# Batch 0's channel output in one 64x64 run per cycle: seventh to ninth cycle of an attention and token/channel mixer kernel

## Chip, cores and metric

The kernel runs on one core of a Trainium2 chip. The metric is the device time of one execution in microseconds (us), the median of several runs. Matmuls run on TensorE (PE in the profile, its weight loads PEld), element-wise work on VectorE (DVE) and ScalarE (ACT), casting loads from memory are issued by GpSimd (POOL), transposing copies and stores by SyncE (SP).

## What is computed

```python
scores = scale * np.matmul(q, k.transpose(0, 1, 3, 2)) - np.log(S)
attn = 1.0 / (1.0 + np.exp(-scores))
x = np.matmul(attn, v)            # then heads side by side: (8, 448, 768)
xt = x.transpose(0, 2, 1)
h = np.maximum(xt @ w_tok1, 0.0) @ w_tok2
u = x + h.transpose(0, 2, 1)
h2 = np.maximum(u @ w_ch1, 0.0) @ w_ch2
return u + h2
```

q, k and v are (8, 12, 448, 64) in float32: 8 batches, 12 heads, 448 positions, head size 64. `w_tok1` is 448x256, `w_tok2` 256x448, `w_ch1` 768x1536, `w_ch2` 1536x768. The output is (8, 448, 768) in float32. The kernel multiplies in fp16 and accumulates in fp32.

## The kernel before

The work is cut into 24 cycles `c`, three per batch (`c = 3*b + u`); a cycle takes four heads. In each cycle seven score steps `qk(b, u, j)` (L182) make the scores of one seventh of the keys in four 64x64 quarters of TensorE, all four at once, and ACT applies the sigmoid and writes `att`. `av` (L208) multiplies the previous cycle's `att` with the values, in quarters too, into two accumulators `xa` that DVE copies to `xu`. `xtrans_dma` (L242) transposes `xu` to `xn` by a transfer on SP's queue. For the cycle two back, `tok_tail` (L267) and `tok1` (L285) are the first token product (the tail in quarters, the rest with the whole 128x128 array; ACT applies the ReLU), and `ytrans` (L312) is the second; DVE adds its two results to `xu`.

With a batch's `xu` complete, the channel products follow. `ch1` (L357, batch 0 only) and `sevens` (L1223, a Strassen-like scheme with seven half-size products named 1 to 7 over three column groups a, b, c) make the hidden layer `h2`; `utrans` (L337) and `token_sums` (L447) prepare it. The second channel product gives the output in groups `(t, half)`: 128 tokens by 384 of the 768 columns, for t = 0, 1, 2, and a last one of 64 tokens for both halves. Before the change batch 0's groups are made by `ch2` (L578): twelve 128x128 matmuls of 384 columns each (L586), then three that add `u` through the identity (L597), then a DVE copy (`ch2_out`, L616). The last one is `ch2_last` (L881): 24 matmuls that use 128 rows and 64 columns of the array (L893) and six that add `u` (L904).

PSUM has eight banks: two tiles of two banks each under the tag `qk` (scores, and products ab of `sevens`), and four banks `m0` to `m3` that `bank()` (L88) hands out, first by a list written out by hand (`OPENING_BANKS`, L27), later from the bank set in `at_bank[0]` on, in turn. A bank or a tile can be written again only when its last reader is done. Every engine runs its instructions in the order in which the program issues them; nothing is reordered.

In the sixth cycle (c = 5) two output groups, (0,0) and (1,0), end the cycle (L1202). In cycles seven to nine (c = 6, 7, 8; from here c6, c7, c8), the loop at L1231, the other four groups and the last one are cut into 20 pieces of three steps; `work(share)` (L1242) puts a third of a cycle's share at each of three places between score steps. With each piece goes one waiting piece of DVE work: a re-layout of q or k (`relayout`, L123, through `through_dma`, L147) or a sum of channel weights (`weight_sums`, L424, twelve of them). c8 ends with `sevens` of batch 1. From c9 on, `steady` (L1315) orders the cycles otherwise: scores, values and quarter products stand together in one run.

Of the kernel before, what the change touches and what calls it, by code (L numbers as in the profile page):

```python
# [21 lines left out]
NJ = 7  # L22
# [1 line left out]
NU = 3  # L24
NS = 224
BY_GROUP = [0, 1, 6, 7, 2, 3, 8, 9, 4, 5, 10, 11]
OPENING_BANKS = "2013013013013021302130213021302131302121302130213020213012"  # L27


@with_exitstack  # L30
def kernel(
# [176 lines left out]
    def av(b, u, j0=0, j1=NJ, banks=None):  # L208
        if j0 == 0:
            xa[b, u] = banks or [  # L210
                bank([128, 512], FP32, f"xa_{b}_{u}_{g}")
                for g in range(2)
            ]
        ps = xa[b, u]
        for j in range(j0, j1):
            for g in range(2):
                for hi in range(2):
                    nc.tensor.matmul(  # L218
                        out=ps[g][64 * hi : 64 * hi + 64, 0:S],
                        lhsT=raw[b, "v"][64 * g : 64 * g + 64, u, hi, j, :],  # L220
                        rhs=att[b, u, j][64 * g : 64 * g + 64, hi, :],
                        start=(j == 0),
                        stop=(j == NJ - 1),
                    )
        if j1 == NJ:
            for g in range(2):
                nc.vector.tensor_copy(  # L227
                    out=xu(b)[:, u, g, 0:S], in_=ps[g][:, 0:S]
                )
            if NU * b + u >= N_CYCLES - 2:  # L230
                nc.vector.memset(xu(b)[:, u, :, S:512], 0.0)
            elif NU * b + u >= N_FIRST:
                nc.vector.tensor_copy(
                    out=xu(b)[:, u, :, S:512], in_=xu(b)[:, u, :, S - 64 : S]
                )
# [188 lines left out]
    def weight_sums():  # L424

        low, high = slice(0, NU), slice(NU, NDB)
        first, second = slice(0, MC), slice(MC, CC)
        s1, s2, s4 = sums

        def one(out, in0, in1, op):  # L430
            return [
                lambda d=d: nc.vector.tensor_tensor(
                    out=out[:, d, :], in0=in0[:, d, :], in1=in1[:, d, :], op=op
                )
                for d in range(NU)
            ]
# [225 lines left out]
        turns = [[lambda t=t, n=n: step(t, n) for n in range(n_quads)] for t in range(2)]  # L662
        return turns[0], turns[1], rest

    def split_steps(ps, n_cb, lhsT, rhs):

        def step(n):
            for r in range(2):
                part = slice(64 * r, 64 * r + 64)
                for m in (0, 64):  # L670
                    nc.tensor.matmul(  # L671
                        out=ps[r][m : m + 64, 0:DH],
                        lhsT=lhsT(part, n, m),
                        rhs=rhs(part, n, m),
                        start=(n == 0),
                        stop=(n == n_cb - 1),
                    )

        return [lambda n=n: step(n) for n in range(n_cb)]
# [475 lines left out]
    for c, cb in ((N_FIRST, 3), (N_FIRST + 1, 8)):  # L1155
        b, u = divmod(c, NU)
        before = divmod(c - 1, NU)
        ahead = divmod(c + 1, NU)
        copies = []

        def whole(cb):
            for d in range(0, NDB, 3):
                ch1(0, cb, d, d + 3)
                if copies:
                    copies.pop(0)()

# [24 lines left out]
        if c - 1 not in ON_DMA:  # L1191
            xtrans(*before)
        for t in ("k", "q"):
            pe_transpose(ahead[0], t, ahead[1])
        whole(cb + 3)
        if c == N_FIRST:
            tok1(*before)
            qk(*ahead, 0)
            whole(cb + 4)
            ytrans(*before)  # L1200
        else:
            for w, f in pieces_ch2(0, by_half[:2]):  # L1202
                f()
                if copies:
                    copies.pop(0)()
            while copies:
                copies.pop(0)()

            nc.gpsimd.tensor_copy(out=gate[:, :], in_=tr[2, "q"][:, 1, NJ - 1, 126:128])
            load(2, "v", v, 1, NU)  # L1210
            gated_loads(b)

    pending, copies = [], []

    def some(n):
        for f in copies[:n]:
# [6 lines left out]
    def sevens(b, banks=(2, 3, 0, 1, 0)):  # L1223
        step = ch1_seven(b, banks)
        for at, (n, gs) in enumerate(SEVENS):
            step(n, gs)
            some((2, 0, 1, 1, 1, 1, 1, 1)[at] if at < 8 else 0)

    early = weight_sums()
    lane = [0]  # L1230
    for c in range(2 * NU, ONE_RUN):  # L1231
        b, u = divmod(c, NU)
        before, ahead = divmod(c - 1, NU), divmod(c - 2, NU)


        if c == 2 * NU:
            first = c
            pending, shares = [*pieces_ch2(0, by_half[2:]), *pieces_last(0)], [10, 10, 10]
            total = sum(w for w, f in pending)
            spent = 0  # L1240

        def work(share):  # L1242
            goal = 3 * sum(shares[: c - first]) + share * shares[c - first]
            done = 0
            while pending and spent + done < total * goal / 90:
                w, f = pending.pop(0)
                if len(pending) % 4 == 3:
                    lane[0] ^= 1
                at_bank[0] = 2 + lane[0]
                f()  # L1250
                done += w
                if copies:
                    copies.pop(0)()
                elif early:
                    early.pop(0)()
            return done

        some(len(copies))
        qk(b, u, 0)
        qk(b, u, 1)  # L1260
        at_bank[0] = 0
        av(*before)
        xtrans_dma(*before)
        qk(b, u, 2)
        if c == 2 * NU + 2:
            copies += through_dma(3, 0)[NU + 1 :]
        spent += work(1)
        qk(b, u, 3)
        qk(b, u, 4)
        if u < 2:  # L1270
            at_bank[0] = 0
            tok_tail(*ahead)
            tok1(*ahead, with_scores=True)
        spent += work(2)
        if c == 2 * NU + 2:
            utrans(b - 1)
            token_sums(b - 1)
            spent += work(3)
        qk(b, u, 5)
        qk(b, u, 6)  # L1280
        at_bank[0] = 0
        if u < 2:
            ytrans(*ahead)
        else:
            tok_tail(*ahead)
            tok1(*ahead, with_scores=True)
        if c == 2 * NU + 1:
            copies += through_dma(3, 0)[: NU + 1]
        if u < 2:
            spent += work(3)  # L1290
        if u == 2:
            assert not copies
            extra = output_sums()
            copies += extra[:8]
            del extra[:8]
            sevens(b - 1)
            at_bank[0] = 0
            ytrans(*ahead)
            gated_loads(b)
    assert not copies and not pending and not early  # L1300

    def more(n):
        for f in extra[:n]:
# [203 lines left out]
```

## Time and profile before

| | |
|---|---|
| median of 3 runs | 340.74 us (340.58 to 341.35) |
| profiled execution | 340.27 us |
| its span, first to last instruction | 338.5 us |
| mean granted TensorE clock | 0.998 |
| DVE busy, share of the span | 235.3 us, 70% |
| ACT busy, share of the span | 212.7 us, 63% |
| POOL busy, share of the span | 61.7 us, 18% |

The span is what the trace covers; 1.77 us of the profiled execution lie around it. In a row of the timeline the columns are: start in us from the span's beginning, length in us, engine, line, operation, what is written and read, tile (for a matmul), shape, count; a row can hold several instructions in a row, and a bracket at the end is the idle time ahead of it with what ended it. Matmuls overlap in the pipeline, so the price of one is the distance from its start to the next one's start, not its length.

### The profile page before, as it was taken

The numbers are of one execution on the slowest core, as the hardware profiler recorded it, in microseconds if no ns is written. First come the engines' busy times: TensorE is split into PE (matmuls) and PEld (weight loads), VectorE is DVE, ScalarE is ACT, GpSimd is POOL, SyncE is SP. The second block draws the span as 40 slices with busy tenths as digits, with TensorE's granted clock in tenths as the row PEclk, the third lists the DMA queues.
The fourth block names the chain that finished last, engine by engine and source line by source line (L and its number), as shares of the span: only waits on it lengthen the run. The fifth ranks groups of instructions, "written<-read, shape, count | busy, mean of one in ns | idle before, by whom it ended". The sixth has DMA issues, their size and how long they took to land.

```text
span 338.5 us, 10318 instructions
## 1 busy us (share of the span) xinstructions
PE 332.2 (98%) x4436; PEld 242.9 (72%) x4436; DVE 235.3 (70%) x486; ACT 212.7 (63%) x272; POOL 61.7 (18%) x108
## 2 busy tenths in 40 slices
PE   8999999999999999999999999999999999999994
PEld 5655556555896679767896679766896679769852
DVE  2376466678998874877668774877768653976882
ACT  4996845388747885678647885678657895314200
POOL 8985380050031002020032001110010000000000
PEclk9999999999999999999999999999999999999999
DMA  8999999999999899989998899988993393028006
GB/s 128 162 160 202 207 178 203 175 175 234 186 179 194 158 171 203 182 125 179 186 190 133 152 151 215 201 123 163 195 179 65 67 171 85 2 56 186 4 13 196
DMA packets 103422, 51.91 MB, mean 153 GB/s; under 512 B 75473, under 2 KB 100305, under 8 KB 103377
## 3 DMA queue, kind: packets, MB, share of 16 engines
q1 hardware_dynamic: 77648, 28.84, 47.0%
q0 software_dynamic: 25264, 21.50, 42.4%
q10 hardware_dynamic: 464, 0.92, 1.0%
q8 instruction: 34, 0.56, 0.6%
q14 instruction: 12, 0.09, 0.1%
HBM read 43.45 MB, written 11.01 MB: 161 GB/s over the span
## 4 chain that ended last, share of the span: by engine, by line
PE 81%; DMA 11%; POOL 5%; DVE 1%; issue 1%; ACT 0%; ACTq 0%; POOLq 0%
PE c_ab L516 14%; PE c L816 10%; PE c_c L516 8%; PE qk L187 8%; PE xa L218 7%; PE c L863 6%; DMA raw_k<-in_k_dram 5%; PE tk L296 4%; PE yt L316 4%; PE c L586 4%; PE c L387 4%; DMA raw_v<-in_v_dram 3%; PE c L671 3%; DMA c<-in_moe_w_ch_dram 3%; PE c L652 2%; POOL raw_q L118 2%
## 5 line engine op out<-in xcount | busy, mean ns | idle before, releaser
L194 ACT ACTIVATE att<-qk,att_bias 128x896 f16<-128x896 f32 x168 | 155.9, 1012 | 37.8 <-PE qk L187 36.7
L187 PE MATMUL qk<-tr_q,tr_k 64*64 64x448 f16 x672 | 60.8, 357 | 0.3 <-DVE tr_k L179 0.2
L516 PEld LDWEIGHTS <-c 128*128 128x128 f16 x504 | 48.4, 98 | 1.1 <-issue 0.3
L218 PE MATMUL xa<-att,raw_v 64*64 64x448 f16 x644 | 40.6, 349 | 0.0
L187 PEld LDWEIGHTS <-tr_k 64*64 64x64 f16 x672 | 25.3, 104 | 18.7 <-issue 11.5
L516 PEld LDWEIGHTS <-sum 128*128 128x128 f16 x378 | 36.3, 98 | 0.0
L227 DVE CAST xu<-xa 128x448 f16<-128x448 f32 x40 | 23.1, 619 | 18.3 <-PE xa L218 17.9
L537 ACT ACTIVATE pt_ab<-c_ab 128x896 f32<-128x896 f32 x21 | 19.2, 917 | 20.6 <-PE c_ab L516 20.6
L218 PEld LDWEIGHTS <-raw_v 64*64 64x64 f16 x672 | 21.9, 107 | 8.2 <-issue 0.4
L863 PE MATMUL c<-c,h 64*64 64x384 f16 x360 | 24.6, 323 | 0.0
L1136 POOL COPY gate<-tr_q 128x2 f16<-128x2 f16 x6 | 1.1, 184 | 121.9 <-DMA tr_q<-rel_q 121.9
L326 DVE TENSOR_TENSOR xu<-xu,yt 128x448 f16<-128x448 f16 x38 | 21.8, 615 | 0.0
L539 ACT ACTIVATE h<-c_ab 128x896 f16<-128x896 f32 x7 | 6.4, 917 | 24.4 <-PE c_ab L516 24.4
L296 PE MATMUL tk<-xn,w 128*128 128x256 f16 x156 | 21.2, 274 | 0.1
L546 DVE TENSOR_TENSOR h<-pt_ab,c_ab 128x896 f16<-128x896 f32 x14 | 15.2, 1083 | 8.6 <-PE c_ab L516 8.6
L546 DVE TENSOR_TENSOR h<-pt_c,c_c 128x448 f16<-128x448 f32 x21 | 12.9, 616 | 11.7 <-PE c_c L516 11.6
L310 ACT ACTIVATE h<-tk 128x256 f16<-128x256 f32 x42 | 14.2, 405 | 9.9 <-PE tk L296 9.9
L316 PE MATMUL yt<-w,h 128*128 128x448 f16 x88 | 20.3, 353 | 0.0
L843 DVE TENSOR_TENSOR o<-un,c 128x384 f32<-128x384 f16 x32 | 17.4, 551 | 4.0 <-PE c L816 4.0
L816 PEld LDWEIGHTS <-hid 128*128 128x128 f16 x132 | 12.9, 98 | 8.0
L516 PE MATMUL c_ab<-diffs,c 128*128 128x224 f16 x168 | 18.4, 259 | 0.0
L118 POOL DMA_DIRECT2D raw_k<-in_k_dram x26 | 16.8, 661 | 8.0 <-DMA c<-in_moe_w_ch_dram 5.6
(132 smaller groups left out, 574.4 us busy)
## 6 DMA issues: line engine op xcount, KB each, us to landing
out_dram<-o SPq DMA_DIRECT2D x41, 192.0 KB, 3.3
c<-in_moe_w_ch_dram POOLq DMA_DIRECT2D x3, 1152.0 KB, 11.6
raw_k<-in_k_dram POOLq DMA_DIRECT2D x10, 336.0 KB, 6.6
raw_q<-in_q_dram POOLq DMA_DIRECT2D x10, 336.0 KB, 5.6
raw_v<-in_v_dram POOLq DMA_DIRECT2D x10, 336.0 KB, 8.2
raw_q<-in_q_dram POOLq DMA_DIRECT2D x16, 112.0 KB, 5.9
raw_k<-in_k_dram POOLq DMA_DIRECT2D x16, 112.0 KB, 6.9
out_dram<-o SPq DMA_DIRECT2D x15, 96.0 KB, 2.4
```

Source lines behind the costliest of these rows:

```text
L118: nc.gpsimd.dma_start(out=dst.rearrange("p u hi j e -> p (u hi) (j e)"), in_=heads.rearrange("h (p j) e -> p h (j e)", j=NJ),)
L187: nc.tensor.matmul(out=ps[64 * g : 64 * g + 64, hi, 0:S], lhsT=tr[b, "k"][64 * hi : 64 * hi + 64, u, j, 64 * g : 64 * g + 64], rhs=tr[b, " ...
L194: nc.scalar.activation(out=att[b, u, j][:, :, :], in_=ps[:, :, 0:S], func=SIGMOID, bias=bias_t[:, :], scale=att_scale,)
L218: nc.tensor.matmul(out=ps[g][64 * hi : 64 * hi + 64, 0:S], lhsT=raw[b, "v"][64 * g : 64 * g + 64, u, hi, j, :], rhs=att[b, u, j][64 * g : ...
L227: nc.vector.tensor_copy(out=xu(b)[:, u, g, 0:S], in_=ps[g][:, 0:S])
L296: nc.tensor.matmul(out=ps[tcb], lhsT=w1[rows, t, cols], rhs=xn[b, u][rows, :, t, :], start=(t == 0 and not with_scores), stop=(t == (2 if ...
L316: nc.tensor.matmul(out=ps[:, 0:S], lhsT=h1[b, u][:, tcb, g, :], rhs=w2[:, tcb, :, :], start=(tcb == 0), stop=(tcb == 1),)
L326: nc.vector.tensor_tensor(out=x, in0=x, in1=ps[:, 0:S], op=ADD)
L516: nc.tensor.matmul(out=ps[:, g, p, :], lhsT=weights[n][:, d, 128 * cb : 128 * cb + 128], rhs=moving[n][:, d, :], start=(n in (1, 5, 2) and ...
L546: nc.vector.tensor_tensor(out=shaped(dst), in0=shaped(parts[gs, which]), in1=ps, op=ADD)
L816: nc.tensor.matmul(out=ps[:, 0:DH], lhsT=self.weights[n][:, k, :], rhs=self.moving[n][:, k, :], start=(n in (1, 2, 5) and k == 0), stop=(k ...
L863: nc.tensor.matmul(out=ps[m : m + 64, 0:DH], lhsT=lhsT(n)[part, m : m + 64], rhs=rhs(n)[part, :], start=(opens and turn == 0 and n == 0), ...
```

## The change

Three new functions make batch 0's output groups out of 64x64 quarters. `first_pair` takes two groups: the first 8 of their 12 steps are done in two turns of eight quarter steps, the rest and the adding of `u` with the whole array. `first_split` does 4 steps of one group in quarters, into two banks, one for each half of the rows; `first_last` does all of the last group in quarters. The calls of a cycle are ordered anew, and the sixth cycle makes one group, (0,0), not two.

```diff
-OPENING_BANKS = "2013013013013021302130213021302131302121302130213020213012"
+OPENING_BANKS = "201301301301302130213021302130213130212130213021302021302"
...
-            for w, f in pieces_ch2(0, by_half[:2]):
+            for w, f in pieces_ch2(0, by_half[:1]):
...
+    def add_u(t, half, ps):
+        for n in range(NU):
+            nc.tensor.matmul(
+                out=ps[:, 128 * n : 128 * n + 128],
+                lhsT=ut(0, NU * half + n)[:, 128 * t : 128 * t + 128],
+                rhs=ident[:, :],
...
+    def plain_rest(t, half, ps, n_quads):
+        for n in range(n_quads, NCB):
+            nc.tensor.matmul(
+                out=ps[:, 0:DH],
+                lhsT=h2[0][:, BY_GROUP[n], 128 * t : 128 * t + 128],
+                rhs=c2[:, BY_GROUP[n], DH * half : DH * half + DH],
...
+        add_u(t, half, ps)
+
+    def first_pair(rows, n_quads):
...
+        ps = [bank([128, 512], FP32, f"c2_0_{t}_{half}") for t, half in rows]
+        turn_bank[0] = ps[1]
...
+        def rest():
+            for p, (t, half) in enumerate(rows):
+                plain_rest(t, half, ps[p], n_quads)
+                ch2_out(0, t, half, ps[p])
...
+    def first_split(t, half, n_quads):
+        ps = [bank([128, 512], FP32, f"c2_0_{t}_{half}_{r}") for r in range(2)]
...
+        def rest():
+            o = outs[0, t][:, cols]
+            nc.vector.tensor_copy(out=o, in_=ps[1][:, 0:DH])
+            plain_rest(t, half, ps[0], n_quads)
+            nc.vector.tensor_tensor(out=o, in0=o, in1=ps[0][:, 0:DH], op=ADD)
+            store(0, t)
...
+    def first_last():
+        ps = [bank([128, 512], FP32, f"c2_0_3_{r}") for r in range(2)]
+        steps = split_steps(
...
+        def end():
+            for n in range(NU):
+                for r in range(2):
+                    part = slice(64 * r, 64 * r + 64)
+                    for m in (0, 64):
+                        nc.tensor.matmul(
+                            out=ps[r][m : m + 64, 128 * n + 64 * r : 128 * n + 64 * r + 64],
+                            lhsT=ut(0, NU * (m // 64) + n)[part, 384:448],
+                            rhs=ident[part, 64 * r : 64 * r + 64],
...
+            nc.vector.tensor_copy(out=o[:, :], in_=ps[0][:, 0:DH])
+            nc.vector.tensor_tensor(out=o[:, :], in0=o[:, :], in1=ps[1][:, 0:DH], op=ADD)
...
         some(len(copies))
         qk(b, u, 0)
         qk(b, u, 1)
-        at_bank[0] = 0
-        av(*before)
-        xtrans_dma(*before)
-        qk(b, u, 2)
...
         if u < 2:
             at_bank[0] = 0
+            av(*before, 0, 5)
+            qk(b, u, 2)
+            at_bank[0] = 2
+            turn0, turn1, rest = first_pair(by_half[1 + 2 * u : 3 + 2 * u], 8)
+            run(turn0, 3)
+            qk(b, u, 3)
+            run(turn0, 5)
+            turn_over(turn_bank[0])
+            av(*before, 5, NJ)
+            xtrans_dma(*before)
+            sums_early(2)
+            qk(b, u, 4)
+            run(turn1, 3)
+            qk(b, u, 5)
+            run(turn1, 5)
+            sums_early(3)
+            at_bank[0] = 0
             tok_tail(*ahead)
+            qk(b, u, 6)
             tok1(*ahead, with_scores=True)
+            rest()
+            at_bank[0] = 0
+            ytrans(*ahead)
+            if u == 1:
+                copies += through_dma(3, 0)[: NU + 1]
+        else:
+            copies += through_dma(3, 0)[NU + 1 :]
+            at_bank[0] = 2
+            steps, end = first_last()
+            run(steps, 7)
+            qk(b, u, 2)
+            run(steps, NCB)
+            end()
+            qk(b, u, 3)
+            at_bank[0] = 0
+            av(*before, 0, 5)
+            qk(b, u, 4)
+            at_bank[0] = 2
+            steps, rest = first_split(2, 1, 4)
+            run(steps, 2)
+            av(*before, 5, NJ)
+            xtrans_dma(*before)
             utrans(b - 1)
             token_sums(b - 1)
+            qk(b, u, 5)
+            run(steps, 2)
+            sums_early(2)
+            at_bank[0] = 0
             tok_tail(*ahead)
+            qk(b, u, 6)
             tok1(*ahead, with_scores=True)
+            some(len(copies))
+            rest()
             extra = output_sums()
             copies += extra[:8]
             del extra[:8]
             sevens(b - 1)
             at_bank[0] = 0
             ytrans(*ahead)
             gated_loads(b)
```

More of the change, by code (lines that the diff above doesn't have):

```diff
@@ L663, in ch2_pair, with split_steps @@
         return turns[0], turns[1], rest
-    def split_steps(ps, n_cb, lhsT, rhs):
+    def split_steps(ps, n_cb, lhsT, rhs, open_ended=()):
         def step(n):
@@ L675, in step @@
                         start=(n == 0),
-                        stop=(n == n_cb - 1),
+                        stop=(n == n_cb - 1 and r not in open_ended),
+                        skip_group_check=bool(open_ended),
                     )
@@ L1211 @@
             gated_loads(b)
-    pending, copies = [], []
+    copies = []
     def some(n):
@@ L1227, in sevens @@
             some((2, 0, 1, 1, 1, 1, 1, 1)[at] if at < 8 else 0)
+    def add_u(t, half, ps):
[4 more added lines that the diff above has]
+                rhs=ident[:, :],
+                start=False,
+                stop=(n == NU - 1),
+                skip_group_check=True,
+            )
+    def plain_rest(t, half, ps, n_quads):
[4 more added lines that the diff above has]
+                rhs=c2[:, BY_GROUP[n], DH * half : DH * half + DH],
+                start=False,
+                stop=False,
+                skip_group_check=True,
+            )
+        add_u(t, half, ps)
@@ new lines, in first_pair, with step @@
+    def first_pair(rows, n_quads):
+        for t, half in rows:
+            if (0, t) not in outs:
+                out_tile(0, t)
+        ps = [bank([128, 512], FP32, f"c2_0_{t}_{half}") for t, half in rows]
+        turn_bank[0] = ps[1]
+        def step(turn, n):
+            quads(
+                ps,
+                DH,
+                turn,
+                lambda p, part, m: h2[0][
+                    part, BY_GROUP[n], 128 * rows[p][0] + m : 128 * rows[p][0] + m + 64
+                ],
+                lambda p, part: c2[
+                    part, BY_GROUP[n], DH * rows[p][1] : DH * rows[p][1] + DH
+                ],
+                n == 0,
+                False,
+                True,
+            )
+        def rest():
+            for p, (t, half) in enumerate(rows):
+                plain_rest(t, half, ps[p], n_quads)
+                ch2_out(0, t, half, ps[p])
+        turns = [[lambda t=t, n=n: step(t, n) for n in range(n_quads)] for t in range(2)]
+        return turns[0], turns[1], rest
@@ new lines, in first_split @@
+    def first_split(t, half, n_quads):
+        ps = [bank([128, 512], FP32, f"c2_0_{t}_{half}_{r}") for r in range(2)]
+        cols = slice(DH * half, DH * half + DH)
+        steps = split_steps(
+            ps,
+            n_quads,
+            lambda part, n, m: h2[0][
+                part, BY_GROUP[n], 128 * t + m : 128 * t + m + 64
+            ],
+            lambda part, n, m: c2[part, BY_GROUP[n], cols],
+            open_ended=(0,),
+        )
+        def rest():
[4 more added lines that the diff above has]
+            store(0, t)
+        return steps, rest
@@ new lines, in first_last @@
+    def first_last():
+        ps = [bank([128, 512], FP32, f"c2_0_3_{r}") for r in range(2)]
+        steps = split_steps(
+            ps,
+            NCB,
+            lambda part, n, m: h2[0][part, BY_GROUP[n], 384:448],
+            lambda part, n, m: c2[
+                part, BY_GROUP[n], DH * (m // 64) : DH * (m // 64) + DH
+            ],
+            open_ended=(0, 1),
+        )
+        def end():
[7 more added lines that the diff above has]
+                            rhs=ident[part, 64 * r : 64 * r + 64],
+                            start=False,
+                            stop=(n == NU - 1),
+                            skip_group_check=True,
+                        )
+            o = last_tile(0)
+            nc.vector.tensor_copy(out=o[:, :], in_=ps[0][:, 0:DH])
+            nc.vector.tensor_tensor(out=o[:, :], in0=o[:, :], in1=ps[1][:, 0:DH], op=ADD)
+            for g in range(2):
+                nc.sync.dma_start(
+                    out=orow[0, NJ - 1][:, DH * g : DH * g + DH],
+                    in_=o[64 * g : 64 * g + 64, :],
+                )
+        return steps, end
@@ L1229 @@
     early = weight_sums()
-    lane = [0]
     for c in range(2 * NU, ONE_RUN):
@@ L1233, with run, sums_early @@
         before, ahead = divmod(c - 1, NU), divmod(c - 2, NU)
[L1236 to L1249, printed above, removed]
-                f()
[L1251 to L1256, printed above, removed]
+        def run(steps, n):
+            for f in steps[:n]:
+                f()
+            del steps[:n]
+        def sums_early(n):
+            for f in early[:n]:
+                f()
+            del early[:n]
         some(len(copies))
@@ L1260 @@
         qk(b, u, 1)
-        at_bank[0] = 0
-        av(*before)
-        xtrans_dma(*before)
-        qk(b, u, 2)
[L1265 to L1269, printed above, removed]
         if u < 2:
             at_bank[0] = 0
+            av(*before, 0, 5)
[15 more added lines that the diff above has]
+            at_bank[0] = 0
             tok_tail(*ahead)
+            qk(b, u, 6)
             tok1(*ahead, with_scores=True)
-        spent += work(2)
-        if c == 2 * NU + 2:
+            rest()
[20 more added lines that the diff above has]
+            xtrans_dma(*before)
             utrans(b - 1)
             token_sums(b - 1)
[L1278 to L1284, printed above, removed]
+            qk(b, u, 5)
+            run(steps, 2)
+            sums_early(2)
+            at_bank[0] = 0
             tok_tail(*ahead)
+            qk(b, u, 6)
             tok1(*ahead, with_scores=True)
[L1287 to L1292, printed above, removed]
+            some(len(copies))
+            rest()
             extra = output_sums()
@@ L1299 @@
             gated_loads(b)
-    assert not copies and not pending and not early
+    assert not copies and not early
     def more(n):
```

## Prediction

> **What bounds the kernel now.** I read the page's busy shares first, then the PE timeline of the cycles that change, then ACT's and DVE's for the same stretch.
>
> ```profile
> PE 332.2 (98%) x4436; PEld 242.9 (72%) x4436; DVE 235.3 (70%) x486; ACT 212.7 (63%) x272; POOL 61.7 (18%) x108
> ```
>
> PE is never free for long, so a microsecond taken from its stream is a microsecond off the end, unless something else then holds it up. The stretch from the end of c5 to the start of c9:
>
> ```profile
> 57.38 1.31 PE L364 MATMUL c<-xu_first,c 128*128 128x448 f16 x6
> 58.83 2.11 PE L586 MATMUL c<-c,h 128*128 128x384 f16 x12
> 60.95 2.11 PE L586 MATMUL c<-c,h 128*128 128x384 f16 x12
> 62.90 0.33 PE L597 MATMUL c<-ident,xu_first 128*128 128x128 f16 x3
> 63.16 0.57 PE L187 MATMUL qk<-tr_q,tr_k 64*64 64x448 f16 x8
> 63.56 1.50 PE L218 MATMUL xa<-att,raw_v 64*64 64x448 f16 x28
> 64.88 0.36 PE L187 MATMUL qk<-tr_q,tr_k 64*64 64x448 f16 x4
> 65.18 1.64 PE L586 MATMUL c<-c,h 128*128 128x384 f16 x9
> 66.74 0.57 PE L187 MATMUL qk<-tr_q,tr_k 64*64 64x448 f16 x8
> 69.76 0.93 PE L316 MATMUL yt<-w,h 128*128 128x448 f16 x4
> 70.53 1.14 PE L586 MATMUL c<-c,h 128*128 128x384 f16 x6
> 71.60 0.57 PE L187 MATMUL qk<-tr_q,tr_k 64*64 64x448 f16 x8
> ...
> 80.21 0.57 PE L187 MATMUL qk<-tr_q,tr_k 64*64 64x448 f16 x8
> 81.93 0.36 PE L187 MATMUL qk<-tr_q,tr_k 64*64 64x448 f16 x4
> 82.22 1.15 PE L586 MATMUL c<-c,h 128*128 128x384 f16 x6
> ...
> 85.95 0.33 PE L904 MATMUL c<-ident,xu_first 128*64 128x128 f16 x6
> 86.21 0.57 PE L187 MATMUL qk<-tr_q,tr_k 64*64 64x448 f16 x8
> ...
> 86.83 0.83 PE L296 MATMUL tk<-xn,w 128*128 128x256 f16 x6
> 87.77 1.31 PE L516 MATMUL c_ab<-xu,c 128*128 128x224 f16 x12
> 90.08 0.74 PE L516 MATMUL c_c<-xu,c 128*128 128x224 f16 x6
> 97.56 1.31 PE L516 MATMUL c_ab<-diffs,c 128*128 128x224 f16 x12
> 100.71 0.57 PE L187 MATMUL qk<-tr_q,tr_k 64*64 64x448 f16 x8
> ...
> 116.59 1.33 PE L671 MATMUL c<-c,h 64*64 64x384 f16 x28
> 117.72 0.39 PE L187 MATMUL qk<-tr_q,tr_k 64*64 64x448 f16 x4
> ```
>
> Prices from starts: a score or value step (four quarters of 448 columns) 0.19 us (28 value matmuls, seven steps, 63.56 to 64.88); a quarter step of 384 columns 0.161 (seven, 116.59 to 117.72); a full matmul of 384 columns 0.1625 (twelve in 58.83 to 60.78, where the first group's L597 begin). Quarters and full matmuls cost the same; a **change of mode** does not come free. The score step at 64.88 is through at 65.07, the next matmul starts at 65.18; nine full ones are through at 66.64, the next starts at 66.74. That is 0.11 and 0.10 us. c6, c7 and c8 each have six such changes.
>
> **ACT and DVE in the same stretch.**
>
> ```profile
> 63.65 2.80 ACT L194 ACTIVATE att<-qk,att_bias 128x896 f16<-128x896 f32 x3 [7.86 <-PE qk L187]
> 86.71 1.90 ACT L194 ACTIVATE att<-qk,att_bias 128x896 f16<-128x896 f32 x2 [0.84 <-PE qk L187]
> ```
>
> A sigmoid starts 0.49 after its score step (63.16 to 63.65), lasts 1.0, and the next follows after 0.90 (three in 2.80). There are two score tiles, so score step 2 waits for sigmoid 0.
>
> ```profile
> 57.57 0.68 DVE L257 COPY xn<-xb 128x1024 f16<-128x1024 f16 x1
> 58.17 0.61 DVE L179 COPY tr_k<-tp_k 128x896 f16<-128x896 f16 x1
> 63.27 0.56 DVE L616 COPY out_first<-c 128x384 f32<-128x384 f32 x1 [1.56 <-PE c L597]
> 66.39 1.49 DVE L432 TENSOR_TENSOR sum<-c 128x768 f16<-128x768 f16 x3
> 70.35 1.15 DVE L326 TENSOR_TENSOR xu<-xu,yt 128x448 f16<-128x448 f16 x2
> 80.03 1.67 DVE L129 COPY rel_k<-raw_k 128x896 f16<-128x896 f16 x3
> 82.14 1.16 DVE L227 CAST xu<-xa 128x448 f16<-128x448 f32 x2 [0.44 <-PE xa L218]
> 83.50 0.62 DVE L129 COPY rel_q<-raw_q 128x896 f16<-128x896 f16 x1
> 85.56 0.22 DVE L339 COPY xu<-xu 128x192 f16<-128x192 f16 x1
> 87.61 1.13 DVE L916 COPY o<-c 64x384 f32<-64x384 f32 x2
> 96.11 1.09 DVE L546 TENSOR_TENSOR h<-pt_ab,c_ab 128x896 f16<-128x896 f32 x1 [0.43 <-PE c_ab L516]
> ```
>
> The reader is to see that DVE in c8 stands nearly still only where a bracket says so: 0.44 and 0.43 us between 80 and 97. It has no room there.
>
> **The change, part by part: gains.** (1) c6, c7 and c8 keep one run of quarters and one of full matmuls each: two changes instead of six, 12 saved, at 0.105: -1.26. (2) The group (1,0) moves out of c5 into c6, one to one; c6 and c7 then make 24 steps each and c8 24. The steps cost the same in both modes: 0. (3) Group (0,0) stands in bank 2 instead of bank 1. Six matmuls of 448 columns from 57.38 are through at 58.53, but L586 starts at 58.83, after the copy out of bank 1 (58.17 + 0.61). Bank 2's last copy (57.57 + 0.68) is done at 58.25: -0.30. (4) In c8 product 1ab needs a score tile whose sigmoid ends at 87.71; `tok1` (six matmuls of 256 columns, 6 x 256/448 x 0.19 = 0.65) is through at 87.48, PE starts at 87.77: 0.28 lost. After, `rest()` stands between: -0.28. (5) `first_last` adds u by 12 matmuls of 64 columns in place of L904's six, which took 0.16 (85.95 to 86.21 less a change). At L904's 0.027 apiece twelve take 0.32: +0.16; if four run at once as the score steps do, nothing (0); if each took the 0.053 of an L597, +0.5. I take +0.16, the rate of the nearest row, and keep 0 to +0.5. Sum: -1.26 - 0.30 - 0.28 + 0.16 = **-1.68**.
>
> **The waits that the new order makes**, each counted from the cycle's first score step.
>
> (6) c6, scores: two score steps 0.40, then five value steps 0.95: PE asks for score tile 0 at 1.35. Sigmoid 0 ends at 1.49, and PE can follow 0.05 later (above, 87.71 to 87.77 is 0.06): wait 0.19. The second score tile is asked for at 1.54 + 0.19 + 0.49 = 2.22, sigmoid 1 ends at 0.49 + 0.90 + 1.0 = 2.39: 0.22. Together **+0.41**. Before, seven value steps stood there (1.72 to 64.88) and covered it.
>
> (7) c7, banks 0 and 1: `ytrans` now ends the cycle, and the next cycle's `av` opens 0.40 after its start in the same two banks. In the row at 69.76 the first addition starts 0.59 behind `ytrans`, and the second ends 1.15 after that. `ytrans` starts 0.86 ahead of the next cycle (0.77 and a change of mode), so the second addition ends at -0.86 + 0.59 + 1.15 = 0.88; the values need it at 0.42. With the handover **+0.52**; the wait of (6) lies inside it and isn't counted for c7. Before, L586 at 70.53 covered it. c6 follows no `ytrans`; c8 opens with `first_last` in banks 2 and 3.
>
> (8) c8, the tail of DVE's list. The two accumulators of the values are complete at 0.40 + 12 x 0.1625 + 0.19 + 0.32 + 0.19 + 0.95 + 0.19 + 0.33 + 0.38 = 4.90; DVE follows 0.21 later (81.93 to 82.14), at 5.11. From there everything stands in a row on DVE: two copies of values and the small one 1.36 (82.14 to 83.50), `utrans` and `token_sums` 2.05 (85.56 to 87.61), two weight sums 0.94 (0.47 each by the row of three), three re-layouts of q 1.59 (0.53 each by the row of three), the copy of one half of group (2,1) 0.56, and the addition of the other 0.6: 12.2. Only then is bank 2 free, and product 1c of `sevens` opens in bank 2: it can start at 12.25. Without waits PE would be there at 9.87 (80.21 to 90.08 before) + 0.98 for six more steps - 0.42 - 0.28 + 0.16 = 10.31: **+1.94**. About 0.9 of it shows early, at `tok_tail`, which now asks for banks 0 and 1 at 5.4, while their copies end at 6.27; the rest at 1c. Queued behind the waiting matmuls is the whole of `sevens`. Afterwards DVE still trails: from the end of L916 (87.61 + 1.13) to product 7ab's addition at 96.11 lie 7.37 us, 6.94 without the 0.43 of idling, 6.3 if smaller gaps in it are as much again and half. From 12.1 on, that addition is then done at 19.5 to 20.1; 4ab needs it at 12.25 + 7.48 (90.08 to 97.56) = 19.7. So nothing is spare: bounds 0 to 0.4 more, and I take 0, since the gaps ahead of additions that follow PE are real.
>
> The Trainium skill, in TensorEngine Tiling (Array Packing), section PSUM Bottleneck, says that tiling speeds TensorE but not the emptying of PSUM, and that both ScalarE and VectorE should be used for that. It is on the side of (7) and (8), where all emptying is VectorE's; with it holding, the sum is the forecast's, without it the first rival's. This trace agrees for c8, by DVE's idle 0.44 and 0.43 us.
>
> Sum: -1.68 + 0.41 + 0.52 + 1.94 = **+1.19** on the span of 338.5: 339.7. The profiled execution took 340.27, 1.77 around its span, and lies 0.47 below the median of 340.74; on that median the forecast is **341.9**. Bounds of the likeliest case: (6) 0 to 0.41, (7) 0.3 to 0.6, (8) 1.4 to 2.4, (5) 0 to 0.5, (3) -0.3 to 0: 341.0 to 342.8.
>
> **Transfers.** The transposes of q for batch 3 leave later: re-layout done at about 11.0 of c8.
>
> ```profile
> 89.53 4.37 SPq L142 DMA_TRANSPOSE tr_q<-rel_q  x1
> 95.96 0.18 POOL L1136 COPY gate<-tr_q 128x2 f16<-128x2 f16 x1 [22.14 <-DMA tr_q<-rel_q]
> ```
>
> It landed 6.4 after its issue. c8 starts at about 79.0 (c5 ends 2.4 earlier, c6 and c7 are 0.7 and 0.6 longer), so issue at 90 to 92 and landing at 96.5 to 98.5; c9 needs it near 102. Cost 0, with 3.5 us of cover; with the cover gone one for one.
>
> **Rivals.** *Mode changes win:* DVE reaches the addition of group (2,1) before PE reaches 1c, so (8) falls to the early 0.3 or less. It decides below a DVE list of 5.2 us from the values to that addition, against 7.1 by the rows. With (6) and (7) it gives -1.68 + 0.93 + 0.3 = -0.45, 340.3; with those hidden too 339.1. For it: DVE is 70% busy. Against: its list has no gap. Chance 0.17. *Waits partly overlap:* (6) and (7) delay PE, so that DVE has caught up, and (8) is 1.2: -1.68 + 0.5 + 1.2, 340.8. Chance 0.20. *Late transfers:* SP's queue, with `utrans` and the stores ahead, delivers xn to c8 or q to c9 too late; it decides from 3.5 us on for q, and each microsecond beyond is one: 343.3 with 1.4. Chance 0.09. *It doesn't do what it says:* the gaps between modes stay elsewhere, as quarters that wait for one another; (1) is 0: 343.2. Against: c9 on has such runs, seven steps at 0.161. Chance 0.06. The forecast has 0.48.
>
> **How the numbers follow.** What a measurement of this kernel tells from no change is about 0.2%, 0.7 us: slower means above 341.4, faster below 340.1. Slower: of the forecast 0.44, of the overlap 0.03, late transfers and lost gains 0.15: 0.62. Faster: 0.13 of the first rival and 0.03 of the second: 0.16. Same: 0.22. The range, 340.0 to 343.0, leaves out half of the first rival and half of the two slow ones, under 0.2 together.
>
> **What would show it.** Right: PE idle of 0.2 twice in c6 ahead of scores; 0.5 at c7's values, ended by DVE L326; in c8 about 0.9 at the token tail, ended by the copies of values, and about 1 at the first c_c matmul of `sevens`, ended by the last addition of batch 0's output; c6 to c8 with one run of 64*64 each; L586 of c5 starting at 58.5. Wrong: `sevens` starting without a gap at c_c, or c9's scores waiting for a transfer.

## The result and the profile after

The changed kernel takes 341.85 us in the median of 6 runs (341.51 to 342.40), the kernel before 340.66 in its 6: ratio 1.0036, 95% interval 1.0022 to 1.0049. It is slower by about 1.2 us. A second set of runs gave 1.0040 (1.0027 to 1.0053). The profiled execution of the changed kernel, 342.40 us with a span of 340.5, was the slowest of its six, so the two traces are compared by the distances within them.

From the page of the changed kernel, the busy shares and the head of the chain that ended last:

```profile
PE 332.7 (98%) x4574; PEld 246.9 (73%) x4574; DVE 236.0 (69%) x489; ACT 212.8 (62%) x272; POOL 62.2 (18%) x108
PE 90%; DVE 3%; ACT 3%; DMA 1%; issue 1%; DVEq 0%
```

The shares tell nothing: PE is at 98% as before. The head of the chain tells little more: ACT's 3% lies between 7.79 and 18.68 us, in the opening, which the change doesn't touch. Most of DVE's 3% (1% before) does belong to it: followed in time, the chain goes over DVE from 69.69 to 71.32, ahead of c7's values, and from 84.54 to 91.62, in c8.

The PE timeline of the changed kernel, with the lines that answer to those shown of before:

```profile
57.90 1.31 PE L364 MATMUL c<-xu_first,c 128*128 128x448 f16 x6
59.04 2.11 PE L586 MATMUL c<-c,h 128*128 128x384 f16 x12
...
61.25 0.57 PE L187 MATMUL qk<-tr_q,tr_k 64*64 64x448 f16 x8
61.66 1.12 PE L218 MATMUL xa<-att,raw_v 64*64 64x448 f16 x20
62.81 0.38 PE L187 MATMUL qk<-tr_q,tr_k 64*64 64x448 f16 x4
62.99 0.68 PE L387 MATMUL c<-c,h 64*64 64x384 f16 x12
63.70 0.38 PE L187 MATMUL qk<-tr_q,tr_k 64*64 64x448 f16 x4
...
70.34 0.57 PE L187 MATMUL qk<-tr_q,tr_k 64*64 64x448 f16 x8
70.83 0.38 PE L218 MATMUL xa<-att,raw_v 64*64 64x448 f16 x2
71.36 1.13 PE L218 MATMUL xa<-att,raw_v 64*64 64x448 f16 x18 [0.15 <-DVE xu L326]
...
79.61 0.57 PE L187 MATMUL qk<-tr_q,tr_k 64*64 64x448 f16 x8
...
82.16 0.28 PE L1326 MATMUL c<-ident,xu_first 64*64 64x64 f16 x10
82.25 0.35 PE L187 MATMUL qk<-tr_q,tr_k 64*64 64x448 f16 x1
...
84.52 0.65 PE L671 MATMUL c<-c,h 64*64 64x384 f16 x8
85.22 0.30 PE L277 MATMUL tk<-xn,w 64*64 64x256 f16 x2
85.75 0.30 PE L277 MATMUL tk<-xn,w 64*64 64x256 f16 x2 [0.23 <-DVE xu L227]
...
86.17 0.83 PE L296 MATMUL tk<-xn,w 128*128 128x256 f16 x6
...
88.30 1.31 PE L516 MATMUL c_ab<-xu,c 128*128 128x224 f16 x12
...
90.03 0.74 PE L516 MATMUL c_b<-xu,c 128*128 128x224 f16 x6
91.66 0.74 PE L516 MATMUL c_c<-xu,c 128*128 128x224 f16 x6 [0.90 <-DVE o L1303]
...
102.29 0.57 PE L187 MATMUL qk<-tr_q,tr_k 64*64 64x448 f16 x8
```

Start to start, c6 takes 9.09 us (before 8.44), c7 9.27 (8.61), c8 with `sevens` 22.68 (20.50). A bracket shows only the time in which no matmul was in flight: for the value products of c7 it says 0.15, while the starts say more, for two of the quarters begin at 70.83 and the rest only at 71.36. A wait is read from the starts, against the price of the work between them.

What ends the waits of c6 and c7 stands in ACT's and DVE's timelines:

```profile
61.75 6.63 ACT L194 ACTIVATE att<-qk,att_bias 128x896 f16<-128x896 f32 x7 [5.44 <-PE qk L187]
```

```profile
70.17 1.14 DVE L326 TENSOR_TENSOR xu<-xu,yt 128x448 f16<-128x448 f16 x2
```

With the prediction's 0.90 from one sigmoid to the next and 1.0 for each, the first of the seven ends at 62.75 and the second at 63.65; the score steps start at 62.81 and 63.70. The additions of `ytrans` end at 71.31; the values that waited start at 71.36.

DVE's timeline of the changed kernel in c8:

```profile
84.54 1.16 DVE L227 CAST xu<-xa 128x448 f16<-128x448 f32 x2 [0.83 <-PE xa L218]
...
88.83 1.66 DVE L129 COPY rel_q<-raw_q 128x896 f16<-128x896 f16 x3
90.41 0.55 DVE L1301 COPY o<-c 128x384 f32<-128x384 f32 x1
91.06 0.55 DVE L1303 TENSOR_TENSOR o<-o,c 128x384 f32<-128x384 f32 x1
```

No later row up to 91.61 has a bracket: DVE works without a pause from the values to the addition that frees bank 2, and PE starts 1c 0.05 us behind it.

The busy time of the engines from the start of c8 to the start of c9, first before, then changed (the columns are the stretch, its length, then busy us and instructions of each engine):

```profile
80.21:100.71 20.50, 20.39 (x237) 16.90 (x236) 18.85 (x39) 12.99 (x18) 3.04 (x5) 1.00 1.10 201
```

```profile
79.61:102.29 22.68, 21.50 (x286) 18.14 (x285) 20.96 (x44) 13.16 (x17) 2.16 (x4) 1.00 1.06 189
```

DVE, the third, has 2.1 us more of work there (two weight sums, one copy more out of PSUM, and most of the additions of `ytrans`, which now run over into c8) and is busy for 92% of the stretch in both. ACT, the fourth, is free for 9.5 of 22.68 us.

### The profile page after: what moved, and what is told of

Its sections match the earlier page's. It is cut to its first block, busy times and chain, and to the rows that moved or that the text cites. A ratio compares the mean times of both kernels' runs of the same rounds, so it can differ in the third digit from the quotient of the medians.

```text
span 340.5 us, 10597 instructions
## 1 busy us (share of the span) xinstructions
PE 332.7 (98%) x4574; PEld 246.9 (73%) x4574; DVE 236.0 (69%) x489; ACT 212.8 (62%) x272; POOL 62.2 (18%) x108
## 4 chain that ended last, share of the span: by engine, by line
PE 90%; DVE 3%; ACT 3%; DMA 1%; issue 1%; DVEq 0%
PE c_ab L516 14%; PE c L817 10%; PE qk L187 10%; PE xa L218 9%; PE c_c L516 8%; PE c L387 6%; PE c L864 6%; PE tk L296 5%; PE yt L316 4%; PE c L671 4%; ACT att L194 3%; PE c L364 3%; PE c L652 2%; DMA first_q<-in_q_dram 1%; PE c_b L516 1%; PE c_a L516 1%
## 5 line engine op out<-in xcount | busy, mean ns | idle before, releaser
L187 PE MATMUL qk<-tr_q,tr_k 64*64 64x448 f16 x672 | 63.1, 356 | 0.3 <-DVE tr_k L179 0.2
L218 PE MATMUL xa<-att,raw_v 64*64 64x448 f16 x644 | 42.0, 349 | 0.2 <-DVE xu L326 0.2
L187 PEld LDWEIGHTS <-tr_k 64*64 64x64 f16 x672 | 26.8, 105 | 18.1 <-issue 10.8
L218 PEld LDWEIGHTS <-raw_v 64*64 64x64 f16 x672 | 22.9, 107 | 8.3 <-issue 1.0
L864 PE MATMUL c<-c,h 64*64 64x384 f16 x360 | 24.6, 323 | 0.0
L387 PE MATMUL c<-c,h 64*64 64x384 f16 x408 | 23.7, 324 | 0.0
L387 PEld LDWEIGHTS <-h 64*64 64x64 f16 x408 | 17.3, 106 | 2.9 <-issue 1.1
```

The costliest lines, as they stand in the source:

```text
L187: nc.tensor.matmul(out=ps[64 * g : 64 * g + 64, hi, 0:S], lhsT=tr[b, "k"][64 * hi : 64 * hi + 64, u, j, 64 * g : 64 * g + 64], rhs=tr[b, " ...
L218: nc.tensor.matmul(out=ps[g][64 * hi : 64 * hi + 64, 0:S], lhsT=raw[b, "v"][64 * g : 64 * g + 64, u, hi, j, :], rhs=att[b, u, j][64 * g : ...
L387: nc.tensor.matmul(out=ps[p][m : m + 64, 0:n], lhsT=lhsT(p, part, m), rhs=rhs(p, part), start=(first and turn == 0), stop=(last and turn = ...
L864: nc.tensor.matmul(out=ps[m : m + 64, 0:DH], lhsT=lhsT(n)[part, m : m + 64], rhs=rhs(n)[part, :], start=(opens and turn == 0 and n == 0), ...
```

## The experiments

Each kernel is read by the same distances as above: c6, c7, c8 with `sevens`, and from the last `ch1` product of c5 to the start of c9, which holds all that changed. The ratios are to the kernel before on the same chip.

| kernel | c6 | c7 | c8 | c5 to c9 | ratio (95%) |
|---|---|---|---|---|---|
| before | 8.44 | 8.61 | 20.50 | 43.33 | 1 |
| changed | 9.09 | 9.27 | 22.68 | 44.39 | 1.0036 (1.0022 to 1.0049) |
| a0_after | 9.08 | 9.28 | 22.68 | 44.40 | 1.0040 (1.0027 to 1.0053) |
| e1_bank | 8.44 | 8.61 | 20.51 | 43.03 | 1.0004 (0.9994 to 1.0015) |
| e2_order67 | 8.95 | 8.82 | 22.68 | 43.80 | 1.0033 (1.0011 to 1.0055) |
| e3_list8 | 9.09 | 9.48 | 21.61 | 43.53 | 1.0009 (0.9995 to 1.0023) |
| e4_all | 8.95 | 8.82 | 22.17 | 43.30 | 1.0021 (0.9996 to 1.0045) |
| e5_bank1c | 9.08 | 9.27 | 22.47 | 44.18 | 1.0031 (1.0022 to 1.0040) |
| e6_modes | 10.01 | 10.19 | 22.68 | 46.23 | 1.0090 (1.0075 to 1.0104) |
| e8_act | 9.09 | 9.27 | 21.62 | 43.33 | 1.0011 (0.9975 to 1.0047) |
| e9_tail | 9.09 | 9.27 | 22.68 | 44.40 | 1.0051 (1.0037 to 1.0064) |
| e7_best | 8.74 | 8.64 | 21.07 | 41.80 | 0.9976 (0.9951 to 1.0001) |
| e7_again | 8.73 | 8.65 | 21.03 | 41.77 | 0.9969 (0.9955 to 0.9984) |

The whole times of one kernel scatter by a microsecond and more; the distances repeat to 0.01 in the changed kernel and to 0.04 in e7_best. a0_after is the changed kernel once more:

> The changed kernel once more, beside the next two. Theory: 1.2 us above the kernel before; c6 9.09, c7 9.27, c8 with sevens 22.7 us. Rival (part of the difference is one of chips or executions): c6 to c8 differ by more than 0.1 us from these.

Its distances are those of the first trace.

**One term alone: the bank of group (0,0).**

```diff
 # the kernel before, last digits of OPENING_BANKS
-...13020213012"
+...13020213023"
```

> The kernel before with the last two digits of the hand-written list alone changed: group (0,0) in bank 2 and (1,0) in bank 3, not 1 and 2. Theory (L586 of c5 waits for the copy out of bank 1): L586 starts 1.14 us after the six matmuls ahead of it, not 1.45, and the whole is 0.3 us under the kernel before (ratio near 0.9991), or less if (1,0) in bank 3 makes a wait of its own. Rival (the start is set by something else, the hidden layer or instruction issue): no difference.

From its PE timeline:

```profile
57.42 1.31 PE L364 MATMUL c<-xu_first,c 128*128 128x448 f16 x6
58.56 2.11 PE L586 MATMUL c<-c,h 128*128 128x384 f16 x12
```

1.14 us, as expected, against 1.45 before, and the distance to c9 is 0.30 shorter. The whole time, 340.32 against 340.65 in the median, doesn't settle it by its interval; the trace does.

**What a change of mode costs.**

```diff
 # the changed kernel; the pair's first group does its four full matmuls
 # singly, between quarter steps of the second turn
+        for k in range(4):
+            turns[1].insert(1 + 3 * k, lambda n=n_quads + k: alone(n))
```

> The changed kernel with the four full matmuls of the pair's first group put singly between quarter steps of the second turn in c6 and c7: the same matmuls, 16 changes of mode more. Theory (a change costs 0.10 to 0.11 us): c6 and c7 each 0.84 longer, the whole 1.7 us above the changed kernel, 2.9 above the kernel before (ratio near 1.0085). Rival (a change costs nothing by itself, and the gaps in the rows are what quarters wait for one another): c6 and c7 as long as in the changed kernel.

c6 and c7 are 0.92 longer each and c8 isn't: 1.84 us for 16 changes, 0.115 each. The price is a change's own. Its PE timeline shows two of them around one full matmul:

```profile
65.02 0.36 PE L387 MATMUL c<-c,h 64*64 64x384 f16 x4
65.31 0.34 PE L1243 MATMUL c<-c,h 128*128 128x384 f16 x1
65.58 0.52 PE L387 MATMUL c<-c,h 64*64 64x384 f16 x8
```

A quarter step of 0.16 is followed after 0.29, a full matmul of 0.16 after 0.27.

**The waits of c6 and c7.**

```diff
 # the changed kernel; c6 and c7
-            av(*before, 0, 5)
-            qk(b, u, 2)
...
+            if u == 0:
+                av(*before, 0, 2)
+                run(turn0, 5)
+            else:
+                run(turn0, 6)
+                av(*before, 0, 1)
+            qk(b, u, 2)
```

> c6 and c7 alone are reordered: c7 opens with six quarter steps of its output pair and then one value step, c6 with two value steps and then five quarter steps, so that both score step 2 and the values come later. The work is the same. Theory (the waits for the sigmoid in c6 and for the additions of ytrans in c7 are lost time): c6 from 9.09 to about 8.7 us, c7 from 9.27 to about 8.7, the whole 0.9 to 1.0 us under the changed kernel, so about 0.2 above the kernel before (ratio near 1.0006). Rival (the waits overlap with DVE's lag in c8, which then grows by as much): c8 longer by 0.5 to 1.0, the whole still 0.8 to 1.2 above the kernel before.

c7 came out at 8.82, c6 only at 8.95. Both parts of c6's wait are gone, but a new one stands further on. Its PE timeline:

```profile
64.60 0.66 PE L387 MATMUL c<-c,h 64*64 64x384 f16 x12
65.37 0.38 PE L187 MATMUL qk<-tr_q,tr_k 64*64 64x448 f16 x4
```

Three quarter steps take 0.49, and 0.77 pass: the sixth score step waits 0.28 for a sigmoid, since the score steps now stand closer together than the 0.90 us that ACT takes for each. Nothing was given back in c8, which stays at 22.68: the expectation's rival, that these waits overlap with DVE's lag, falls. The gain of 0.59 in the distances is less than the 0.9 expected by that new wait and some 0.1 in c7; the whole time shows at most a part of it, within its interval.

**The length of DVE's list in c8.**

```diff
 # the changed kernel; weight sums three and three in c6 and c7, none in c8
-            sums_early(2)
...
-            some(len(copies))
             rest()
+            some(len(copies))
+            store(0, 2)
```

> c8 alone: the two weight sums go to c6 and c7 (three and three there), and the three re-layouts of q go behind the addition of group (2,1), whose store follows them. DVE's list from the values to that addition is 2.5 us shorter; its total in c8 is 0.9 shorter. Theory (bank 2, freed by that addition, holds 1c): the wait of 1.06 us at the first c_c product is gone, start of c8 to start of c9 from 22.7 to about 21.6, the whole 1.0 under the changed kernel, about 0.1 to 0.2 above the kernel before; the 0.9 at the token tail stays. Rival (DVE trails anyway, the order within its list doesn't matter): the wait moves to product 4ab, and at most 0.3 is won. Rival (late transfers): c9's scores wait for the transposes of q.

c8 takes 21.61, as expected. The two rows of its PE timeline:

```profile
89.78 0.74 PE L516 MATMUL c_b<-xu,c 128*128 128x224 f16 x6
90.36 0.74 PE L516 MATMUL c_c<-xu,c 128*128 128x224 f16 x6
```

0.58 from 2b to 1c, no wait. c7 became 0.2 longer instead: with one more sum ahead of them, c6's copies and additions end later, and c7's values wait for those.

> The changed kernel with two pieces of c8's DVE list on ACT, which idles there: the copy of group (2,1)'s first half out of PSUM, and the first re-layout of q. DVE's list is 1.1 us shorter, its order stays. Theory (bank 2 waits for the length of DVE's list): the wait of 1.06 ahead of 1c is gone or under 0.1, c8 with sevens 21.6, the whole 1.0 under the changed kernel. Rival (ACT then is late for the ReLUs or for 1ab's part, and PE waits there): c8 longer than 22.

```diff
 # the changed kernel
-            nc.vector.tensor_copy(out=o, in_=ps[1][:, 0:DH])
+            nc.scalar.activation(out=o, in_=ps[1][:, 0:DH], func=COPYF)
...
+            relayout(3, "q", 0, on_scalar=True)
+            del copies[0]
             some(len(copies))
```

c8 again loses 1.06, by moving 1.1 us of DVE's work to ACT and nothing else, so what counts is the length of the list up to the addition that frees bank 2, however it is cut. The prediction named the Trainium skill, TensorEngine Tiling (Array Packing), section PSUM Bottleneck: PSUM is to be emptied by ScalarE as well as VectorE. This trace agrees, 22.68 to 21.62, though only half of what moved empties PSUM; the other half is a re-layout.

**Which bank, and what stands behind it.**

```diff
 # the changed kernel, batch 1's sevens in c8
-            sevens(b - 1)
+            sevens(b - 1, (3, 2, 0, 1, 0))
```

> The changed kernel with banks 2 and 3 exchanged in batch 1's sevens alone: 1c opens in bank 3, which the copy of group (2,1)'s first half frees, 0.65 us ahead of the addition that frees bank 2. DVE's list is the same. Theory (bank release holds 1c, and DVE's whole list holds 4ab behind it): 1c starts 0.65 earlier, 4ab then waits for 7ab's addition about 0.4; net 0.2 to 0.3, so 0.9 to 1.0 above the kernel before. Rival (the bank alone): the whole 0.65 is won, 0.5 above the kernel before. Rival (1c waits for something else): 1c starts where it did.

Two rows of its PE timeline:

```profile
90.91 0.74 PE L516 MATMUL c_c<-xu,c 128*128 128x224 f16 x6 [0.24 <-DVE o L1301]
...
98.84 1.31 PE L516 MATMUL c_ab<-diffs,c 128*128 128x224 f16 x12 [0.29 <-DVE h L546]
```

1c starts 11.40 after c8 and not 12.05, released by the copy. Product 4ab, which follows 3ab after 1.15 in the changed kernel, follows it after 1.61 here (97.23 to 98.84): of the 0.65 won, 0.46 are lost to the additions of `sevens`. The net is 0.21. Freeing 1c's bank earlier wins little while DVE's list stays as long as it was.

**One lag or two waits.**

```diff
 # the changed kernel
-            steps, rest = first_split(2, 1, 4)
+            steps, rest = first_split(2, 1, 8)
...
-            run(steps, 2)
+            run(steps, 6)
+            qk(b, u, 6)
             sums_early(2)
             at_bank[0] = 0
             tok_tail(*ahead)
-            qk(b, u, 6)
```

> The changed kernel with the token tail of c8 alone moved behind six quarter steps of group (2,1) and the last score step (that group with eight quarter steps, four full matmuls fewer): PE has 1.3 us of work between the values and the tail, as long as their copies out of banks 0 and 1 take. DVE's list is as in the changed kernel. Theory (the 0.9 at the tail and the 1.06 at 1c are one lag of DVE, counted from the values): the wait at the tail is gone, 1c still starts 12.0 to 12.1 us after c8, so it now waits 1.9, and c8 with sevens stays at 22.7. Rival (two waits of their own): c8 with sevens 21.8.

```profile
85.83 0.43 PE L277 MATMUL tk<-xn,w 64*64 64x256 f16 x4
87.68 1.31 PE L516 MATMUL c_ab<-xu,c 128*128 128x224 f16 x12
...
91.81 0.73 PE L516 MATMUL c_c<-xu,c 128*128 128x224 f16 x6 [1.67 <-DVE o L1303]
```

In this PE timeline the four tail matmuls stand together without a wait, `sevens` begins 0.77 earlier from c8's start than in the changed kernel (7.92 against 8.69), and 1c starts 12.05 after c8 as there. c8 stays at 22.68. The two waits of c8 are one lag of DVE, counted from the values.

**All waits, two attempts.** The first took everything at once:

> The changed kernel with all three kinds of wait taken away: c6 and c7 as in e2_order67, c8's DVE list as in e3_list8, one re-layout of q put into DVE's idle 0.8 us ahead of the values; group (2,1) with all eight quarter steps, six of them ahead of the token tail; two output sums fewer during sevens (made in c9); the transposing copy of u behind that of q. The same work throughout. Theory (the waits of 0.41, 0.5, 0.9 and 1.06 are all that stands against the gains of 1.7): 2.5 to 2.9 us under the changed kernel, 1.3 to 1.7 under the kernel before (ratio 0.995 to 0.9965). Rival (DVE's total work holds c8 whatever the order): 4ab or c9 waits for DVE, and the whole is within 0.5 of the kernel before. Rival (late transfers): c9's scores wait for q.

```diff
 # c6, c7 as e2_order67; c8 as e3_list8 and e9_tail, and
             end()
+            some(1)
...
-            copies += extra[:8]
+            copies += extra[:6]
```

It missed: c8 takes 22.17, and the ratio, 1.0021, isn't told from 1. Its DVE timeline has the reason:

```profile
83.17 0.55 DVE L1341 TENSOR_TENSOR o<-o,c 128x384 f32<-128x384 f32 x1
85.42 0.62 DVE L129 COPY rel_q<-raw_q 128x896 f16<-128x896 f16 x1 [1.69 <-DMA raw_q<-in_q_dram]
85.95 1.15 DVE L227 CAST xu<-xa 128x448 f16<-128x448 f32 x2
```

The one re-layout put into DVE's idle time found q not yet landed, waited 1.69 us, and held the values' copies behind it by 1.4. Also, c10 took 7.69 (7.22 in the changed kernel), presumably by the two more output sums that stand on DVE's list at the end of c9; that was not tried alone.

The second attempt:

```diff
 # c6, c7 as e2_order67, with
-            run(turn1, 3)
-            qk(b, u, 5)
-            run(turn1, 5)
+            run(turn1, 5)
+            qk(b, u, 5)
+            run(turn1, 3)
 # and two weight sums each ahead of turn0, behind turn_over and behind xtrans_dma;
 # c8 as e8_act and e9_tail, re-layouts and store as e3_list8, no sums
+            send_un()
```

> All waits taken on together, by what the runs so far show: c6 and c7 as in e2_order67, but with the sixth score step two quarter steps later (there it waited 0.28 us for a sigmoid) and the weight sums in DVE's idle time ahead of and behind the small copy; c8 with both pieces of e8_act on ACT, the other re-layouts behind the addition of group (2,1), all eight quarter steps of that group with six ahead of the token tail, no re-layout before the values (in e4_all it waited 1.7 us for q to land), output sums as in the changed kernel. Theory: c6 and c7 8.7 each, c8 with sevens 20.9 to 21.1, the way from the last ch1 product of c5 to c9 41.6 to 41.9 us (before 43.3, changed kernel 44.4), the whole 1.2 to 1.7 under the kernel before (ratio 0.995 to 0.9965). Rival (DVE's total work holds 4ab or c9): c8 with sevens above 21.5. Rival (late transfers): c9's scores or its first output additions wait for q or u.

> The same kernel as e7_best once more, for a narrower interval on its time. Theory: 0.9 to 1.5 us under the kernel before, c6 8.7, c7 8.65, c8 with sevens 21.1.

The distance from c5 to c9 is 41.80 and 41.77 us, 2.6 under the changed kernel and 1.5 under the kernel before. The trace names no wait for DVE in c6 to c8; about 0.2 us are still lost at the token tail of c8, which takes 0.58 up to `tok1` (84.65 to 85.23) against 0.36 in e9_tail (85.83 to 86.19), and what holds it there isn't shown. The whole is 0.9976 (0.9951 to 1.0001) and 0.9969 (0.9955 to 0.9984) of the kernel before, 339.86 and 339.59 in the median against 340.79 and 340.92. In the second set the interval lies under 1, in the first it just reaches it: 0.2 to 0.3% less than the kernel before, 0.6% less than the changed one. The windows of c8 with `sevens` in the first run:

```profile
78.57:99.64 21.07, 21.04 (x298) 18.43 (x297) 19.24 (x41) 14.28 (x19) 2.84 (x5) 1.00 1.09 190
```

DVE has 1.7 us less to do than in the changed kernel's 22.68, ACT 1.1 more, and PE is busy in all but 0.03.

## Why the prediction was right

The forecast was +1.2 us, 341.9; measured 341.85. The mechanism was right: the waits that the new order makes cost more than the changes of mode that it saves. The parts:

- **Changes of mode (1).** Taken at 0.105, 16 of them cost 0.115 each (e6_modes). The twelve saved are worth 1.3 to 1.4.
- **Bank of (0,0) (3).** 0.30 predicted; 1.45 to 1.14 from the six matmuls to L586, and 0.30 in e1_bank alone.
- **1ab (4).** It starts at 88.30, 0.16 behind the last three u matmuls (88.14, three at 0.053): no wait. As predicted.
- **Adding u in `first_last` (5).** Mis-sized. The twelve small matmuls begin at 82.16 and the next score step at 82.25: about 0.1 us for all, not 0.32. That is the prediction's case of four at once, and just under its bound of 0: the step costs 0.06 less than before, not 0.16 more.
- **c6 (6).** Five value steps from 61.66 should end at 62.61; the score step starts at 62.81. Three quarter steps from 62.99 should end at 63.48; it starts at 63.70. 0.20 and 0.22, of 0.19 and 0.22 predicted.
- **c7 (7).** 9.27 less the 8.67 that c6's like work takes without its waits (9.09 - 0.42): 0.60, of 0.52 predicted; e2_order67 and e7_best without that wait need 8.82 and 8.64.
- **c8 (8).** At the tail 86.17 - 84.52 less 0.74 of work (two quarter steps, tail, score step and change of mode) leaves 0.9; at 1c 91.66 - 90.03 - 0.57 = 1.06: 1.96, of 1.94 predicted. 1c starts at 12.05 and not 12.25, since (5) came out 0.2 shorter ahead of the values. That it is one list of DVE's is shown by e8_act (shorter: 1.06 won) and e9_tail (the first wait taken away: nothing won).
- **Behind c8.** "Nothing is spare" at 4ab was right within 0.3: 7ab's addition ends at 98.88 (97.80 + 1.08), 4ab starts at 99.14, and e5_bank1c, 0.65 earlier, lost 0.46 there. The row of before at 90.06 has a third bracket, 0.26, that the prediction's reading of DVE's pauses left out; its lower estimate of 6.3 us allows for as much.

From c5 to c9 that makes 44.39 - 43.33 = +1.06, where the same terms foretold 1.2 (1.0 with (5) at what it measured). That the whole time agrees to 0.05 is luck: (5) was 0.2 too dear, and from the start of c9 on came 0.1 (by the medians) to 0.4 us (by the traces), where the prediction had no term. The bounds, 341.0 to 342.8, are narrower than the terms' own bounds, which add up to 340.6 to 343.1; how they were narrowed isn't said.

The rivals: *mode changes win* falls because DVE's list took 7.07 us (84.54 to 91.61), not the 5.2 below which it decides. The overlap falls by e2_order67, and that the mode changes bring nothing falls by e6_modes. Late transfers didn't show in the changed kernel, but the way there was partly wrong: on SP's queue the transposes of q stood behind that of u (issued at 90.83) and left at 94.63, 15.0 into c8, where the prediction had 11 to 13. They landed by 99.80, when GpSimd's copy that waits for them ran, for a start at 102.29: 2.5 us of the 3.5 of cover were left.

Open: from the start of c9 to the end of the span the traces of the changed kernel and its variants take 238.0 to 238.7 us, the kernel before and e1_bank 237.8. In the changed kernel the matmuls up to the last group take as long as before (102.29 to 333.24, against 100.71 to 331.64); the difference stands behind the issue of the last store. From ACT's queue, before and changed:

```profile
334.53 0.50 ACTq L925 DMA_DIRECT2D out_dram<-o  x1
```

```profile
336.13 0.50 ACTq L926 DMA_DIRECT2D out_dram<-o  x1
```

With spans of 338.5 and 340.5 that is 3.97 and 4.37 us. The last two stores, 96 KB each, land 2.6 and 2.4 us after issue before (2.7 and 2.5 in e1_bank) and 3.1 and 2.8 in the changed kernel (2.8 to 3.1 and 2.6 to 3.2 in all traces of the new order). Those eleven traces also have an instruction transfer of 0.02 MB after 326 us, which the other two don't; whether it delays the stores isn't shown. The difference stands beside the 1.06 in the measured difference, and it takes that much from the gain of e7_best.

## What to carry over

An interleave that looks inefficient on the busy engine may be what hides the others: before PE's work is sorted by mode, list what each wait of the new order will find, score tile by score tile and bank by bank. A secondary engine's list from its last input to the freeing of a bank is a path of its own. Its busy share doesn't show whether it holds the main engine (DVE was busy for 92% of c8 before and after); its length against the main engine's way to that bank does, 7.1 us against 5.2 here. Shorten the list or share it with an idle engine, for moving the wait (e5_bank1c, e9_tail) wins little or nothing. A gap of an engine is no free place until the data of what is put there is known to have landed.

## What the runs showed of the hardware

Twelve matmuls of 64x64 on 64 columns in four quarters took about 0.1 us together (82.16 to 82.25), under 0.01 each, a third of the 0.027 of L904's, which have twice the columns. And the length of a load is not fixed: that of q for batch 3, two issues of 336 KB, landed 8.8 us after issue in the median before, 9.2 in the changed kernel and 10.1 in e4_all, where its early re-layout met it.
